# Constant products before the first attention block, a second bank and a later order for the products with v, and an earlier place for three attention blocks

## The chip, the cores and the metric

The kernel runs on one core of a Trainium2 chip. The metric is the device time of one execution in microseconds. One core has a matrix engine (PE), a vector engine (DVE), a scalar engine (ACT), GpSimd (POOL) and a queue engine (SP) that issues most transfers; each works through its own list in order and waits for the others by semaphores.

## What is computed

Three stages follow each other: causal attention with a decay, a layer norm with a two-layer MLP and a residual, and a gated MLP that mixes over the sequence. All of it is float32 with 4 batches, 8 heads, 576 positions and a head width of 64.

```python
scores = scale * np.matmul(q, k.transpose(0, 1, 3, 2))
decay = cum[:, :, :, None] - cum[:, :, None, :]          # cum: running sum of log f
scores = np.where(causal, -1e9, scores + decay)
attn = softmax(scores);  x = attn @ v                    # (4, 576, 512)
xn = (x - mu) / np.sqrt(var + 1e-06) * g_ln
x = x + np.maximum(xn @ w_ch1, 0.0) @ w_ch2              # 512 -> 2048 -> 512
h = np.maximum(x @ w_in, 0.0);  u, v = halves of h       # 512 -> 1024
out = (u * (w_spatial @ norm(v) + b_spatial)) @ w_out
```

## The kernel before

**Blocks.** The tokens are cut into eight blocks of 256 (`BLOCKS`, numbered 0 to 7) and the last 64 positions of each batch. Blocks 0 and 1 hold the first 128 positions of two batches each (`attention32`, float32 throughout), blocks 2 and 3 the next 128 (`attention1`), blocks 4 to 7 the positions from 256 on, one batch each (`attention`). Attention of each block goes over four pairs of heads (`p`, called pair 0 to 3 here). For each block the MLP follows as a group (`mlp`, numbered 0 to 7): sixteen rounds over tiles of the two weight matrices, L700 for the first product and L685 for the second. Group 0 runs in float32 while the weights are still being converted; the later ones in pairs of float16 parts.

**A pair of heads in `attention32`.** Scores (L352, four products into bank `acc`), row minimum on DVE (L355), exponentials on ACT (L357), the reciprocal of the sums and a diagonal matrix of it on DVE (L361, L365), a product with that (L369, bank `ph`) that transposes and scales, a copy on ACT (`PT`, L370), the product with v (L377, bank `av`, of which there is one) and its copy on ACT (`xT`, L378). After the fourth pair DVE adds the parts (`ls`), PE makes their mean (L603), and the norm and the first MLP group follow.

**A pair of heads in `attention`.** `weights(i, heads)` makes the scores of one tile of 128 rows (L293), the exponentials, and two float16 parts `P` on ACT (L258) and DVE (L314, the last of them); a transposing transfer writes them to `PT`. `values` multiplies with v (L456, thirty products) and is put, for one pair, behind the first tile's weights of the second head of the pair after it; for the last pair at the block's end.

**Weights.** Float64 weights arrive as 64-bit words (`raw`, 1 MB for each of sixteen tiles, three buffers). `narrow` makes float32 of them: ACT takes the high word (L525) and the low word (`low`, L526), DVE puts them together (L527 to L529), and PE makes sums of squares for the scales (`gram`, L561).

**What sets the order.** The program is written as an ordered list of events, each with a place in units of groups. `SPAN[n]` is the stretch in which block n's attention is placed, `BEGIN` the start of each group, `CONV` the conversions of the first weight tiles, `PACE` after what each conversion's first instruction is put. A scheduler then orders the instructions of each engine by its own timeline; `self.after(later, earlier)` forces one behind the other in that order without a wait at run time.

Of the kernel before, what the change touches and what calls it, by code (L numbers as in the profile page):

```python
# [9 lines left out]
BF16 = mybir.dt.bfloat16  # L10
I64 = mybir.dt.int64
U32 = mybir.dt.uint32
I32 = mybir.dt.int32
# [5 lines left out]
P = 128  # L19
# [18 lines left out]
W8 = 1  # L38
RAWB = 3
AHEAD = 2  # L40

# [7 lines left out]
E0, E1 = -0.1, 0.45  # L49
SPAN = [(-1.0, -0.6), (0.02, 0.45), (0.46, RAMP - 0.42), (RAMP - 0.4, RAMP - 0.1)]  # L50
for _n in range(4):
# [3 lines left out]
CONV = (-0.6, 0.001, 0.002, 0.003, 0.004)  # L55
PACE = (1, "split", "split", "split", "split")
SUMS = 13
SOON = 5
# [25 lines left out]
class Kernel:  # L84
# [194 lines left out]
    def weights(self, i, heads):  # L279
# [29 lines left out]
        for k0, k1 in pieces:  # L309
            w = P if k1 * P <= N else R  # L310
            src = sd[:M, k0 * P : k0 * P + (k1 - k0 - 1) * P + w].rearrange("p (t w) -> p t w", w=w)
            dh, dl = ph[:M, k0:k1, 0, :w], ph[:M, k0:k1, 1, :w]
            self.copy(DHE[i - 2], dh, src, rs)
            nc.vector.scalar_tensor_tensor(out=dl, in0=src, scalar=rs, in1=dh, op0=ALU.mult, op1=ALU.subtract)  # L314
        for u, (_, PT) in enumerate(heads):
            tr = nc.sync.dma_start_transpose(out=PT[:, : 2 * nb, qs], in_=ph[R * u : R * u + R, :nb].rearrange("p t h w -> p (t h w)"))
            self.in_order("tr", tr)


    def attention32(self, b, xT):  # L320
# [25 lines left out]
        for p in range(NP):  # L346
# [24 lines left out]
            if not b:  # L371
                self.done.append(copied)
            pav = bank(tags[2])
            for n in range(2):
# [65 lines left out]
    def attention(self, b, xT, xt):  # L440
# [5 lines left out]

        def values(p, vp, vsc, heads):

            pav = self.bank("av")
            for kt in range(5):  # L450
                n0 = max(kt * P, q0) - q0
                kr = min(P, S - kt * P)
                for vi, pi in ((0, 1), (1, 0), (0, 0)):
                    for u in range(2):
                        us = slice(64 * u, 64 * u + 64)
                        nc.tensor.matmul(  # L456
                            pav[us, n0:W], lhsT=vp[:kr, vi, kt, us], rhs=heads[u][1][:kr, 2 * kt + pi, n0:W],
                            start=(kt == 0 and (vi, pi) == (0, 1)), stop=(kt == 4 and (vi, pi) == (0, 0)), skip_group_check=True)
            nc.scalar.activation(xT[:, p, :], pav[:, :TOK], AF.Copy, scale=vsc)
            nc.scalar.activation(xt[:, p, :], pav[:, TOK:W], AF.Copy, scale=vsc)  # L460
            if p == 1:
                self.xs = self.mo_sum(xT)
            elif p == 2:
                nc.vector.tensor_tensor(out=self.xs, in0=self.xs, in1=xT[:, 2, :], op=ALU.add)
# [3 lines left out]
        for p in range(NP):  # L468
            heads = []
            for u in range(2):  # L470
# [7 lines left out]
                for i in (2, 3):  # L478
                    self.weights(i, heads[u:])
                    if late and (u, i) == (1, 2):  # L480
                        yield
                        values(*late)
                    yield
# [28 lines left out]
    def narrow(self, raw, tmp, low=None):  # L512
# [10 lines left out]
        else:  # L523

            first = nc.scalar.activation(a, words(raw, 1, F32), AF.Abs, scale=2.0**16)  # L525
            nc.scalar.activation(low.bitcast(I32), lo, AF.Copy, scale=LOW)  # L526
            nc.vector.tensor_scalar(out=a, in0=a, scalar1=F64_LO * 2.0**16, scalar2=F64_HI * 2.0**16, op0=ALU.max, op1=ALU.min)  # L527
# [14 lines left out]
    def load_w(self, j):  # L542
# [7 lines left out]
        if at is not None:  # L550
            self.after(first, self.marks[at] if isinstance(at, str) else self.done[at])

    def squares(self, j):
# [449 lines left out]
    def run(self):  # L1003
# [18 lines left out]
        at_cm = self.pool("at0", side="right")  # L1022
        self.at = at_cm.__enter__()
        with self.pool("dk") as dk:
            self.decays(dk)
# [208 lines left out]
```

## Time and profile before

| | us |
|---|---|
| median of three runs (lowest, highest) | 810.4 (809.69, 812.69) |
| the profiled execution, its own time | 811.59 |
| its span, first to last instruction | 809.9 |
| PE busy | 766.2 (95%) |
| DVE busy, ACT busy | 554.8 (69%), 516.7 (64%) |

A row of a timeline gives the start, the length, the engine with its line and the tiles written and read; in brackets stands how long the engine was idle before it and what ended that. Float32 products show two records each, so a row "x8" of L352 is the four products of one pair. Rows of one engine overlap a little, because products are pipelined: what a row takes in a stream is the distance from its start to the next row's. The granted clock of PE stands in the tables by stretch; 1.00 is 2.4 GHz and 0.50 is 1.2 GHz.

### The profile page before, as it was taken

What the parts mean: (1) busy time and instruction counts of PE and PEld (TensorE: products, weight loads), DVE (VectorE), ACT (ScalarE), POOL (GpSimd) and SP (SyncE); (2) the same over time, 40 slices, a digit from 0 to 9 for tenths busy, and PEclk for the clock granted to TensorE, in tenths of its full rate; (3) what the DMA queues carried; (4) which work ended last, traced back from release to release, by engine and by line L of the source; (5) the groups of instructions that cost most, each with busy time, mean ns of one, the idle gap of its engine ahead of it and who ended that gap; (6) DMA issues with size and microseconds to landing.
All of it is one profiled execution on the core that took longest, in us unless ns stands there. A gap on an engine that the chain in (4) does not pass through costs nothing.

```text
span 809.9 us, 16194 instructions
## 1 busy us (share of the span) xinstructions
PE 766.2 (95%) x5924; PEld 582.1 (72%) x5924; DVE 554.8 (69%) x1502; ACT 516.7 (64%) x1303; POOL 59.7 (7%) x89
## 2 busy tenths in 40 slices
PE   4889998999889999999999999999999999999997
PEld 4678887777777777877778788644447667667676
DVE  4479769938479988979757963778435563664735
ACT  4488668839478988878767862576325644656542
POOL 3000011001110101101101100100012000000000
PEclk9989999999999999999999999999999999999999
DMA  8578758336778998998787675651024230000101
GB/s 251 135 256 303 245 167 153 76 95 143 123 208 174 202 209 157 181 198 181 155 153 154 110 117 146 162 172 53 0 48 77 67 118 1 30 30 4 57 2 58
DMA packets 164226, 104.71 MB, mean 129 GB/s; under 512 B 106178, under 2 KB 151362, under 8 KB 164148
## 3 DMA queue, kind: packets, MB, share of 16 engines
q1 hardware_dynamic: 157848, 96.63, 49.0%
q0 software_dynamic: 5296, 5.28, 5.1%
q10 hardware_dynamic: 1004, 1.78, 0.8%
q8 instruction: 46, 0.75, 0.4%
q14 instruction: 32, 0.26, 0.1%
HBM read 64.37 MB, written 15.11 MB: 98 GB/s over the span
## 4 chain that ended last, share of the span: by engine, by line
PE 65%; DMA 11%; DVE 10%; ACT 9%; issue 3%; SPq 2%; POOL 1%; ACTq 0%; DVEq 0%; POOLq 0%
PE ph L700 14%; PE acc L685 13%; PE pb L640 8%; PE pb L641 8%; PE pb L642 8%; DMA PT<-P 5%; PE s L293 3%; PE av L456 3%; DMA vr<-in_v_dram 2%; DVE wt L593 2%; PE av L377 1%; PE s L685 1%; ACT x L258 1%; ACT P L258 1%; DMA raw<-in_moe_w_in_dram 1%
## 5 line engine op out<-in xcount | busy, mean ns | idle before, releaser
L685 PE MATMUL acc<-hh,wt 128*128 128x256 f16 (+2 forms) x960 | 196.7, 295 | 1.0 <-ACT hh L707 1.0
L700 PE MATMUL ph<-xh,wt 128*128 128x256 f16 (+1 forms) x896 | 185.6, 288 | 3.1 <-DVE hl L711 3.1
L700 PEld LDWEIGHTS <-wt 128*128 128x128 f16 x1344 | 126.9, 98 | 48.1 <-issue 9.6
L685 PEld LDWEIGHTS <-wt 128*128 128x128 f16 x1344 | 128.7, 98 | 44.7 <-issue 6.1
L700 PE MATMUL ph<-xl,wt 128*128 128x256 f16 (+1 forms) x448 | 129.0, 288 | 0.0
L685 PE MATMUL acc<-hl,wt 128*128 128x256 f16 (+1 forms) x416 | 115.4, 281 | 0.0
L707 ACT ACTIVATE hh<-ph 128x256 f16<-128x256 f32 (+2 forms) x128 | 51.0, 399 | 51.5 <-PE ph L700 51.3
L711 DVE SCALAR_TENSOR_TENSOR hl<-ph,hh 128x256 f16<-128x256 f32 (+1 forms) x112 | 50.5, 453 | 41.2 <-ACT hh L707 40.9
L258 ACT ACTIVATE P<-sd,st 128x512 f16<-128x512 f32 (+2 forms) x128 | 70.9, 586 | 8.0 <-DVE st L304 4.6
L301 ACT ACTIVATE sd<-sd,st 128x384 f32<-128x384 f32 (+2 forms) x80 | 54.6, 682 | 18.0 <-DVE st L297 17.8
L293 PE MATMUL s<-x 68*128 68x384 f32 (+7 forms) x256 | 63.3, 359 | 1.4 <-ACT sd L301 1.0
L314 DVE SCALAR_TENSOR_TENSOR P<-sd,st,P 128x384 f16<-128x384 f32 (+2 forms) x96 | 58.3, 625 | 8.7 <-ACT P L258 7.2
L297 DVE CUSTOM_DVE_ANT_0 sd<-s,mask 128x384 f32<-128x384 f32 (+2 forms) x80 | 46.0, 581 | 8.7 <-PE s L293 7.7
L732 POOL DMA_DIRECT2D x_d<-t x36 | 32.4, 1082 | 195.3 <-DVE t L728 169.5
L258 ACT ACTIVATE x<-qk 64x320 fp32r<-64x320 f32 (+1 forms) x64 | 41.6, 697 | 3.3 <-DMA qk<-in_qk_dram 2.0
L456 PE MATMUL av<-PT,vp 128*64 128x320 f16 (+2 forms) x480 | 33.9, 270 | 8.1 <-DMA PT<-P 6.4
L293 PEld LDWEIGHTS s<-x 68*128 68x128 f32 (+3 forms) x256 | 36.8, 177 | 4.3 <-ACT sd L301 1.2
L456 PEld LDWEIGHTS <-vp 128*64 128x64 f16 (+1 forms) x480 | 24.5, 109 | 19.5 <-issue 10.6
L983 DVE SCALAR_TENSOR_TENSOR u<-pb,wsc,u 128x288 f32<-128x288 f32 x32 | 15.9, 514 | 32.9 <-PE pb L982 32.9
L642 PE MATMUL pb<-x2h,wih 128*128 128x288 f16 (+2 forms) x144 | 37.8, 273 | 0.0
L640 PE MATMUL pb<-x2h,wil 128*128 128x288 f16 (+2 forms) x144 | 37.8, 273 | 0.0
L641 PE MATMUL pb<-x2l,wih 128*128 128x288 f16 (+2 forms) x144 | 37.8, 273 | 0.0
(275 smaller groups left out, 1619.8 us busy)
## 6 DMA issues: line engine op xcount, KB each, us to landing
raw<-in_moe_w_ch_dram SPq DMA_DIRECT2D x32, 512.0 KB
qk<-in_qk_dram SPq DMA_DIRECT2D x32, 448.0 KB
vraw<-in_v_dram SPq DMA_DIRECT2D x5, 1024.0 KB
vr<-in_v_dram SPq DMA_DIRECT2D x16, 320.0 KB
x_d<-xT SPq DMA_DIRECT2D x9, 512.0 KB
x_d<-t POOLq DMA_DIRECT2D x36, 128.0 KB, 4.3
out_dram<-o SPq DMA_DIRECT2D x32, 144.0 KB
raw<-in_moe_w_in_dram SPq DMA_DIRECT2D x8, 512.0 KB
```

The lines of the kernel that those rows point to most:

```text
L258: self.nc.scalar.activation(out, in_, AF.Copy, scale=scale)
L293: nc.tensor.matmul(ps[: R * u + R, : c1 - c0], lhsT=x[:, lo - q0 - R * u : hi - q0], rhs=y[:, c0:c1], start=g == 0, stop=g == len(heads[u] ...
L301: nc.scalar.activation(sd[:M, :N], sd[:M, :N], AF.Exp, bias=st[:M, n : n + 1], scale=-1.0, accum_out=st[:M, 2:3])
L314: nc.vector.scalar_tensor_tensor(out=dl, in0=src, scalar=rs, in1=dh, op0=ALU.mult, op1=ALU.subtract)
L456: nc.tensor.matmul(pav[us, n0:W], lhsT=vp[:kr, vi, kt, us], rhs=heads[u][1][:kr, 2 * kt + pi, n0:W], start=(kt == 0 and (vi, pi) == (0, 1) ...
L640: first = mm(out, lhsT=al, rhs=bh, start=start, stop=False, **kw)
L641: mm(out, lhsT=ah, rhs=bl, start=False, stop=False, **kw)
L642: mm(out, lhsT=ah, rhs=bh, start=False, stop=stop, **kw)
L685: ins = nc.tensor.matmul(acc[m], lhsT=a, rhs=b, start=bank not in clear, stop=last and e == len(terms) - 1, skip_group_check=True)
L700: ins = nc.tensor.matmul(ph, lhsT=a, rhs=b, start=k == e == 0, stop=k == NK - 1 and e == len(terms) - 1)
L707: relu = nc.scalar.activation(hh, ph, AF.Relu)
L711: nc.vector.scalar_tensor_tensor(out=hl, in0=ph, scalar=0.0, in1=hh, op0=ALU.max, op1=ALU.subtract)
```

## The change

There are five edits. **Constant products:** ahead of everything else on PE, 54 products of a tile of ones with itself (bfloat16, 128 by 128 against 256 columns) go into bank `s2`; nothing reads them. **Second bank:** in block 0, pairs 1 and 3 put the product with v into `s2` instead of `av`. **Later values:** in `attention`, the products with v of one pair are put behind DVE's last instruction (L314) of the first tile's weights of the second head of the next pair. **Low words:** the low-word conversions of weight tiles 0, 1 and 2 are put behind the copies `PT` of pairs 1, 2 and 3 of block 0 (`self.done`). **Places:** `SPAN` of block 1 ends 0.1 group sooner, blocks 2 and 3 begin 0.1 sooner, and blocks 4 to 7, whose places follow from block 3's end, 0.08 sooner.

```diff
+WARM = 54
-SPAN = [(-1.0, -0.6), (0.02, 0.45), (0.46, RAMP - 0.42), (RAMP - 0.4, RAMP - 0.1)]
+SPAN = [(-1.0, -0.6), (0.02, 0.35), (0.36, 0.98), (1.0, 1.32)]
+LOWAT = (1, 2, 3)
@@ weights
-            nc.vector.scalar_tensor_tensor(out=dl, in0=src, scalar=rs, in1=dh, op0=ALU.mult, op1=ALU.subtract)
+            low = nc.vector.scalar_tensor_tensor(out=dl, in0=src, scalar=rs, in1=dh, op0=ALU.mult, op1=ALU.subtract)
...
+        return low
@@ attention32
-            pav = bank(tags[2])
+            pav = bank("s2" if p % 2 and not b else tags[2])
@@ attention
-        def values(p, vp, vsc, heads):
+        def values(p, vp, vsc, heads, behind=None):
...
+                        if behind is not None and kt == 0 and (vi, pi) == (0, 1):
+                            self.after(ins, behind)
...
-                    self.weights(i, heads[u:])
+                    done = self.weights(i, heads[u:])
                     if late and (u, i) == (1, 2):
                         yield
-                        values(*late)
+                        values(*late, done)
@@ narrow
-            nc.scalar.activation(low.bitcast(I32), lo, AF.Copy, scale=LOW)
+            self.low = nc.scalar.activation(low.bitcast(I32), lo, AF.Copy, scale=LOW)
@@ load_w
+        if j < len(LOWAT):
+            self.after(self.low, self.done[LOWAT[j]])
@@ run
+        warm, ones = self.bank("s2"), self.ones.bitcast(BF16)
+        for i in range(WARM):
+            self.nc.tensor.matmul(warm[:, : 2 * P], lhsT=ones[:, :P], rhs=ones, start=True, stop=True)
```

The order of the instructions shows three places; a row that only repeats one above it is left out. The lines of the changed kernel are numbered a little higher: L352, L357, L369, L370, L377 and L526 of before are L355, L360, L372, L373, L380 and L531 there, L293 and L456 are L295 and L459, and L700 and L685 are L707 and L692.

PE from its first instruction, before: the scores of the four pairs of block 0, the transposing products of pairs 0 and 1, pair 0's products with v, pair 2's transposing products, the first scores of block 1 (`s2_447`) and pair 1's products with v.

```order
L352 MATMUL acc_169<-qk_151 128x128 x4
L352 MATMUL acc_201<-qk_151 128x128 x4
L352 MATMUL acc_235<-qk_151 128x128 x4
L352 MATMUL acc_268<-qk_151 128x128 x4
L369 MATMUL ph_187<-diag_171,e_170 128x128 x4
L369 MATMUL ph_219<-diag_203,e_202 128x128 x4
L377 MATMUL av_195<-PT_188,vr_152 128x128
L377 MATMUL av_195<-PT_188,vr_152 64x128
L369 MATMUL ph_253<-diag_237,e_236 128x128 x4
L352 MATMUL s2_447<-qk_431 128x128 x4
L377 MATMUL av_227<-PT_220,vr_152 128x128
L377 MATMUL av_227<-PT_220,vr_152 64x128
```

PE in the changed kernel, from the last of the 54 constant products on:

```order
L1033 MATMUL s2_93<-ones_62 128x256
L355 MATMUL acc_224<-qk_206 128x128 x4
L355 MATMUL acc_256<-qk_206 128x128 x4
L355 MATMUL acc_290<-qk_206 128x128 x4
L355 MATMUL acc_323<-qk_206 128x128 x4
L372 MATMUL ph_242<-diag_226,e_225 128x128 x4
L372 MATMUL ph_274<-diag_258,e_257 128x128 x4
L380 MATMUL av_250<-PT_243,vr_207 128x128
L380 MATMUL av_250<-PT_243,vr_207 64x128
L372 MATMUL ph_308<-diag_292,e_291 128x128 x4
L380 MATMUL s2_282<-PT_275,vr_207 128x128
L380 MATMUL s2_282<-PT_275,vr_207 64x128
```

The constant products stand ahead, and where block 1's scores stood behind pair 2 there are now pair 1's products with v, in the second bank, with pair 2's right behind; block 1's scores have gone behind the last product of block 0, just ahead of the mean.

ACT in block 0, before, from the exponentials of pair 1 on (`low` and `wt` are the conversions, `raw_160` the first weight tile):

```order
L357 ACTIVATE e_202,st_204<-e_202,st_204 128x128 x4
L526 ACTIVATE low_322<-raw_160 128x1024
L360 ACTIVATE st_204<-st_204 128x4
L357 ACTIVATE e_236,st_238<-e_236,st_238 128x128 x4
L360 ACTIVATE st_238<-st_238 128x4
L370 ACTIVATE PT_188<-ph_187 128x512
L526 ACTIVATE low_342<-raw_163 128x1024
L357 ACTIVATE e_269,st_271<-e_269,st_271 128x128 x4
L370 ACTIVATE PT_220<-ph_219 128x512
L525 ACTIVATE wt_146<-raw_160 128x1024
L378 ACTIVATE xT_150<-av_195 128x256
L360 ACTIVATE st_271<-st_271 128x4
```

ACT in the changed kernel, from the same exponentials on:

```order
L360 ACTIVATE e_257,st_259<-e_257,st_259 128x128 x4
L363 ACTIVATE st_227<-st_227 128x4
L360 ACTIVATE e_291,st_293<-e_291,st_293 128x128 x4
L363 ACTIVATE st_259<-st_259 128x4
L363 ACTIVATE st_293<-st_293 128x4
L373 ACTIVATE PT_243<-ph_242 128x512
L360 ACTIVATE e_324,st_326<-e_324,st_326 128x128 x4
L373 ACTIVATE PT_275<-ph_274 128x512
L530 ACTIVATE wt_201<-raw_215 128x1024
L531 ACTIVATE low_377<-raw_215 128x1024
L363 ACTIVATE st_326<-st_326 128x4
L381 ACTIVATE xT_205<-av_250 128x256
```

The first low word, which stood right behind the exponentials of pair 1, has gone behind the copy `PT` of pair 1, with the high word now ahead of it; the exponentials of pairs 2 and 3 and two copies `PT` stand ahead of both.

PE at the first product with v of pair 0 of block 4, before (`av_2668`; `s_2752` are scores of pair 1's last tile, in the middle of MLP products):

```order
L685 MATMUL acc_2477<-hh_3176,wt_146 128x256
L685 LDWEIGHTS wt_146
L685 MATMUL acc_2477<-hl_3177,wt_146 128x256
L456 LDWEIGHTS vp_2504
L456 MATMUL av_2668<-PT_2304,vp_2504 64x320
L293 MATMUL s_2752<-x2_2536 128x288
L293 MATMUL s_2752<-x1_2535 128x288
L293 MATMUL s_2752<-x2_2402 64x288
L293 MATMUL s_2752<-x1_2401 64x288
L685 MATMUL acc_2478<-hl_3177,wt_146 128x256
```

PE at the same product in the changed kernel (`av_2648`; `s2_2809` are scores of the next tile, of another head):

```order
L295 MATMUL s2_2809<-x2_2592 128x384
L295 MATMUL s2_2809<-x1_2591 128x384
L707 LDWEIGHTS wt_201
L707 MATMUL ph_3470<-xl_2607,wt_201 128x256
L707 MATMUL ph_3470<-xh_2606,wt_201 128x256
L692 LDWEIGHTS wt_201
L692 MATMUL acc_2608<-hl_3379,wt_201 128x256
L692 MATMUL acc_2608<-hh_3378,wt_201 128x256
L459 LDWEIGHTS vp_2462
L459 MATMUL av_2648<-PT_2301,vp_2462 64x320
L459 MATMUL av_2648<-PT_2366,vp_2462 64x320
```

The products with v (rows 2559 to 2618 of that list) now stand behind that next head's scores and five MLP products, and no longer in the middle of the last tile's scores.

## Rows read from the trace of the kernel before

**Rows 1.** busy time by stretch: us, busy us of PE, PEld, DVE, ACT, POOL, granted clock, DMA

```profile
50.00:100.00 50.00, 50.00 (x330) 43.30 (x329) 45.48 (x76) 38.56 (x72) 0.00 (x0) 1.00 0.80 278
```

**Rows 2.** PE's timeline: start us, length us, line, tiles, records, idle time before and its releaser

```profile
10.13 5.49 PE L352 MATMUL acc<-qk 66*128 66x128 f32 x24 [10.13 <-DMA qk<-decay]
16.08 2.05 PE L352 MATMUL acc<-qk 66*128 66x128 f32 x8 [0.46 <-DVE st L355]
...
21.56 2.05 PE L369 MATMUL ph<-diag,e 128*128 128x128 f32 x8 [1.73 <-DVE st L361]
23.40 2.60 PE L377 MATMUL av<-PT,vr 128*128 128x128 f32 x8
25.93 2.08 PE L369 MATMUL ph<-diag,e 128*128 128x128 f32 x8
28.43 2.05 PE L352 MATMUL s<-qk 66*128 66x128 f32 x8 [0.42 <-DMA qk<-decay]
...
32.80 1.03 PE L561 MATMUL gram<-wt 128*128 128x128 bf16 x8
...
38.26 1.63 PE L377 MATMUL av<-PT,vr 128*128 128x128 f32 x8 [0.47 <-ACT xT L378]
40.83 1.22 PE L603 MATMUL av<-ls,onesf 128*128 128x256 f32 x2 [0.93 <-DVE ls L614]
...
48.83 0.63 PE L561 MATMUL gram<-wt 128*128 128x128 bf16 x8 [0.83 <-DVE wt L529]
...
57.23 1.10 PE L369 MATMUL s<-diag,e 128*128 128x128 f32 x8
58.18 1.06 PE L352 MATMUL s<-qk 66*128 66x128 f32 x8
...
76.10 1.53 PE L377 MATMUL av<-PT,vr 128*128 128x128 f32 x8
```

**Rows 3.** busy time by microsecond, columns as in Rows 1, around the clock's first fall and rise

```profile
40.00:41.00 1.00, 0.17 (x1) 0.18 (x2) 0.42 (x1) 0.31 (x1) 0.00 (x0) 0.90 0.17 14
41.00:42.00 1.00, 1.00 (x2) 0.33 (x2) 0.00 (x0) 0.00 (x0) 0.00 (x0) 0.50 1.13 100
...
47.00:48.00 1.00, 0.98 (x2) 0.50 (x2) 0.96 (x2) 1.00 (x2) 0.00 (x0) 0.69 0.50 71
```

**Rows 4.** the chain of waits: start us, length us, what

```profile
9.34 6.62 DMA raw<-in_moe_w_ch_dram
```

**Rows 5.** ACT's timeline behind the exponentials of pair 1 of block 0

```profile
18.22 1.12 ACT L526 ACTIVATE low<-raw 128x1024 int32<-128x1024 uint32 x1 [2.11 <-DMA raw<-in_moe_w_ch_dram]
```

**Rows 6.** DVE's timeline at the kernel's start: the tile of ones

```profile
1.05 0.17 DVE L134 MEMSET ones<- 128x128 f32 x1
```

**Rows 7.** groups of ACT by line between 10 and 40 us: count, busy, mean ns

```profile
L357 ACT ACTIVATE e<-e,st 128x128 f32<-128x128 f32 x16 | 6.2, 390 | 2.8 <-DVE st L355 2.8
L526 ACT ACTIVATE low<-raw 128x1024 int32<-128x1024 uint32 x3 | 3.4, 1125 | 2.1 <-DMA raw<-in_moe_w_ch_dram 2.1
...
L370 ACT ACTIVATE PT<-ph 128x512 f32<-128x512 f32 x4 | 2.4, 590 | 4.0 <-PE ph L369 4.0
```

**Rows 8.** groups of DVE by line between 10 and 40 us

```profile
L528 DVE SCALAR_TENSOR_TENSOR low<-raw,low 128x1024 uint32<-128x1024 uint32 x3 | 3.7, 1221 | 2.8 <-ACT low L526 2.8
L365 DVE TENSOR_TENSOR diag<-ident,st 128x512 f32<-128x512 f32 x4 | 2.8, 688 | 0.1
...
L529 DVE SCALAR_TENSOR_TENSOR wt<-wt,low 128x1024 uint32<-128x1024 uint32 x1 | 1.2, 1195 | 0.0
```

**Rows 9.** waits of PE between 100 and 460 us: total, times, longest

```profile
PE av L456 <- DMA PT<-P: 6.4, 7, 1.7
PE av L428 <- DMA PT<-P: 4.6, 3, 1.7
```

**Rows 10.** PE's timeline: products with v of pair 3 of blocks 5 and 6

```profile
353.73 0.32 PE L456 MATMUL av<-PT,vp 128*64 128x320 f16 x1 [0.68 <-DMA PT<-P]
...
420.36 0.30 PE L456 MATMUL av<-PT,vp 128*64 128x320 f16 x1 [1.22 <-DMA PT<-P]
```

More of the change, by code (lines that the diff above doesn't have):

```diff
@@ L455, in values @@
                         us = slice(64 * u, 64 * u + 64)
-                        nc.tensor.matmul(
+                        ins = nc.tensor.matmul(
                             pav[us, n0:W], lhsT=vp[:kr, vi, kt, us], rhs=heads[u][1][:kr, 2 * kt + pi, n0:W],
                             start=(kt == 0 and (vi, pi) == (0, 1)), stop=(kt == 4 and (vi, pi) == (0, 0)), skip_group_check=True)
+                        if behind is not None and kt == 0 and (vi, pi) == (0, 1):
+                            self.after(ins, behind)
             nc.scalar.activation(xT[:, p, :], pav[:, :TOK], AF.Copy, scale=vsc)
```

## The prediction

> **What bounds the kernel now.** I read the table by stretch first. From 50 to 100 us PE is busy without a gap [rows 1], while the start has limits of its own. PE's own list bounds the kernel, so time comes only from work that PE does before its unbroken stream, and from gaps in it. The stream starts at 48.83 us and the mean ahead of it at 40.83 us; the 8.0 us between are a chain through DVE, ACT and PE that the change leaves alone [rows 2]. So I ask when the mean of block 0 can start, and then what becomes of PE's gaps.
>
> Next is PE's timeline of the start. Three pairs' scores take 5.49 us from 10.13, or 1.83 for each; a pair's transposing products take 1.84 at 21.56 and its products with v 2.53 at 23.40, from one row's start to the next. Rows of the same sets later last 1.06, 1.10 and 1.53 us, where these last 2.05, 2.05 and 2.60 [rows 2]. So PE runs at half speed here, 1.2 GHz. The granted clock reads 1.00 until its first recorded fall to 0.50, between 40 and 41 us, and comes back between 47 and 48 us [rows 3]; before 40 us I go by the lengths, and by them the clock rises once, shortly before the row of 38.26 us, whose 1.63 us are nearly the fast 1.53. Ahead of that rise PE had worked from 28.43 to 37.8 us. The 5.49 us of scores from 10.13 had not raised it, nor had the run from 21.56 to 28.0 [rows 2].
>
> Third are the gaps at the start. Pair 3's scores begin at 16.08 us; the bracket names DVE, but the chain has a transfer landing at 9.34 + 6.62 = 15.96 us there [rows 2, 4]. ACT stood 2.11 us at the first low word, waiting for weights, and gave 1.12 us to it [rows 5], ahead of pair 1's sums; PE lost 1.73 us before 21.56 for this. Another 0.47 us went before 38.26 for the single bank `av` [rows 2].
>
> **The constant products.** The trace has no such product. In `gram`, 128 columns eight times take 1.03 us at the low clock and 0.63 at the high one [rows 2], tails of 0.2 us included, so 256 columns are about 0.21 or 0.11 us (estimates). All 54 would take 11.3 or 5.9 us. They can start at about 1.3 us, when the ones are written [rows 6]. With a rise 4 to 6 us later some 19 to 28 are slow, and they end between 9 and 10.2 us, beside transfers that hold PE until 10.13 anyway [rows 2]. Cost nothing, then; 2.5 us of delay for the first scores if the clock never rose. What they buy is that the first scores run at the high clock.
>
> **Does the clock stay?** Pairs 0 and 1 then need 2.1 us from 10.13; pair 2 ran at 10.13 + 2 x 1.83 = 13.8 in before, and pair 3 still waits for 16.0. PE is thus half idle between 12 and 16 us. In before the clock fell at 40.9 us behind gaps of 0.47 and 0.93 us, with PE busy for 0.17 of its last microsecond [rows 2, 3]. By that row I take it that the clock is lost between 13 and 17 us. The Trainium skill (TensorE: Matmul & The Clock Gate, HAM oscillation) shows the clock lost to waits of 3 to 5 us between bursts. None of the gaps here would be that long, and by it the clock would stay high all through, which is rival (b). The fall at 40.9 us speaks against it.
>
> **The mean of block 0, two bounds.** From 16.0 us on PE has one set of scores, four transposing sets, four with v, one `gram` and block 1's first scores. At the low clock that is 1.83 + 4 x 1.84 + 4 x 2.53 + 0.84 + 1.83 = 22.0 us, so the mean starts at 38.0. This holds if nobody keeps PE waiting: the low word and its wait now stand behind `PT` of pair 1, and `s2` takes pairs 1 and 3. At the high clock PE's work is 11 to 12 us, and another chain is later. Pair 3's exponentials cannot begin before 17.3; ACT has four of them at 0.39 us, two `PT` of 0.59 and the high and low word of 1.12 each [rows 7], to 22.3. DVE's L528, L529 and the diagonal follow, 1.22 + 1.20 + 0.69 [rows 8], to 25.4. Then come PE's 0.95, `PT` 0.59, PE's 1.45, the copy `xT` and the sum, some 0.4 each (estimates, `PT` is twice as wide), with nine hand-overs at about 0.15 us: the mean at about 31.
>
> Between them: PE works from 16.0 without a break in this order, and a run of 9 us from 28.43 brought the clock up. So it rises at about 25; 9 of 22 us are done by then, the other 13 take 7, which gives 32, and ACT's chain adds about 1. I take **33.1**, against 40.83: **7.7 us sooner**, of bounds 2.8 and 9.8. A part may be lost again: the norm's chain leaves PE mostly idle, so the stream may start at the low clock, where in before the rise came just ahead of it. I take 1.0 us back (bounds 0 and 2, half of up to 4 us).
>
> **The stream.** In it the MLP rows and block 1's pairs keep their order to within a few products, and loads and conversions go by its pace, so I carry the whole shift through. DVE is busy 45.5 of 50 us there [rows 1], close, but PE has no gap.
>
> **Later values.** PE waited 6.4 us, seven times, for `PT` at products with v in blocks 4 to 7, at most 1.7 us [rows 9]. In the new order the first three pairs of each block have 1.9 to 9.3 us more of PE work between their last scores and the products with v, 4.7 in the mean (PE's order, summed with the durations of the rows). The mean is well above the longest wait, so those waits are gone; the last pair of a block keeps its place and its wait, 0.68 and 1.22 us of the 6.4 [rows 10]. I take **4.5 us** (bounds 0 and 6.4).
>
> **Places.** In block 2 two products with v now stand 1.4 and 2.0 us closer behind their scores. Transfers of `PT` held three such products for 4.6 us in before [rows 9], so closer ones can wait: I take **1.5 us** as loss (bounds 0 and 3.4). The other moves change no distance by as much; cost nothing, within 1.5 either way.
>
> Sum: 7.7 - 1.0 + 4.5 - 1.5 = 9.7 us. The profiled execution took 811.6 us, 1.7 of them outside its span, and would become 801.9; it stands 1.2 above the median of 810.4, against which I predict **800.7**.
>
> **Rivals.** (a) *The clock stays low until 38 us:* sets with v ran in the stretches that did not raise it. Then the mean comes at 38.0, 2.8 sooner, with nothing lost at the stream: 2.8 + 4.5 - 1.5 = 5.8, **804.6**. (b) *It stays high from the constant products on,* because the gaps are short: the mean at 31, 9.8 + 4.5 - 1.5 = 12.8, **797.6**. (c) *The constant products do not raise it:* they end at 12.6 us, pairs 0 to 2 follow at the low clock until 18.1, pair 3 until 19.9 in place of 17.8, the mean is at 40.1: 0.7 + 4.5 - 1.5 = 3.7, **806.7**. (d) *Slower:* products with v that come later also free `PT` later. If the transposing transfers of the pair after next wait for that, SP's queue stands with every load behind it, and each of twelve moved products meets a wait. At 1.7 us, the longest seen [rows 9], that is 20.4 us in place of the 4.5 gained: 7.7 - 1.0 - 1.5 - 20.4 = -15.2, **825.6**. It decides the sign from 5.2 / 12 = 0.4 us for each. Against it speaks that two pairs of `PT` alternate and the products still stand ahead of the weights that reuse them.
>
> **How the numbers follow.** The forecast gets 0.50, (a) 0.22, (b) 0.14, (c) 0.08, (d) 0.06. About 0.5%, 4.1 us, is what a measurement can tell from no change here, so faster means below 806.3. Nearly all of the forecast, whose unknown costs put it at 797 to 805.5, (b), and three quarters of (a) lie below: 0.81 faster, 0.13 within, 0.06 slower. The range holds the forecast, (b) with no loss in block 2 (796.1) and (a) with half of the values' gain (806.9): 795.5 to 807.5.
>
> **What would show it.** Right: 54 products that end before 10.2 us and get shorter on the way; scores of pairs 0 and 1 in about 1.05 us each; no wait of ACT at the first low word; the mean near 33 us and the stream's first `gram` near 41; waits for `PT` at the values' line of about 2 us in place of 6.4. Wrong: a mean at 38 us (the clock) or at 31 (it stayed), a stream that starts earlier but has new gaps, or waits on SP's queue for the products with v.

## The result: about 9 us faster, near the forecast, for reasons that were partly others

| | kernel before | changed kernel |
|---|---|---|
| median, same job | 811.55 us (809.69 to 813.18, 4 runs) | 801.67 us (800.36 to 804.47, 4 runs) |
| ratio to before | 1 | 0.9884, interval 0.9846 to 0.9922 |
| profiled execution, its span | 811.6, 809.9 us | 800.8, 799.1 us |
| mean of block 0 starts | 40.83 us | 31.35 us |
| first transposing set inside the stream | 57.23 us | 49.09 us |
| PE waits for `PT` at the values' line | 6.4 us, 7 times | 2.2 us, once |
| PE waits for anything at that line | 8.1 us, 9 times | 4.9 us, 3 times |
| PE waits for `PT` at attention1's products with v | 4.6 us, 3 times | 0.3 us, once |

The forecast was 800.7 us, with a range of 795.5 to 807.5. All lines of the changed kernel stand a few numbers lower down: L355 are the scores (L352 before), L372 the transposing products, L380 block 0's products with v, L459 the later blocks' (L456), L610 the mean (L603), L707 and L692 the MLP, L1033 the constant products.

PE's timeline of the changed kernel's start, columns as in [rows 2]:

```profile
8.76 0.49 PE L1033 MATMUL s<-ones 128*128 128x256 bf16 x3
10.16 2.05 PE L355 MATMUL acc<-qk 66*128 66x128 f32 x16 [0.91 <-DMA qk<-decay]
12.72 1.13 PE L355 MATMUL acc<-qk 66*128 66x128 f32 x8 [0.51 <-DVE st L358]
14.26 1.13 PE L355 MATMUL acc<-qk 66*128 66x128 f32 x8 [0.41 <-DVE st L358]
16.24 3.75 PE L372 MATMUL ph<-diag,e 128*128 128x128 f32 x16 [0.85 <-ACT e L360]
19.79 2.60 PE L380 MATMUL av<-PT,vr 128*128 128x128 f32 x8
22.32 1.16 PE L372 MATMUL ph<-diag,e 128*128 128x128 f32 x8
...
30.22 1.16 PE L355 MATMUL s<-qk 66*128 66x128 f32 x8
31.35 0.67 PE L610 MATMUL av<-ls,onesf 128*128 128x256 f32 x2
...
39.01 0.77 PE L568 MATMUL gram<-wt 128*128 128x128 bf16 x8 [1.12 <-DVE wt L534]
39.57 3.53 PE L707 MATMUL ph<-xg,wt 128*128 128x256 f32 x8
...
45.12 1.94 PE L707 MATMUL ph<-xg,wt 128*128 128x256 f32 x8
46.90 1.89 PE L692 MATMUL acc<-hh,wt 128*128 128x256 f32 x8
```

All four pairs' scores are done by 15.4 us, where before pair 3 began only at 16.08 [rows 2]. From 16.24 on PE goes through four pairs almost without a break, and block 1's first scores come behind all of them instead of ahead of pair 1's products with v. The row of 39.57 has eight records, which are four MLP products, in 3.53 us; in the next round, at the high clock, four take 1.94, or 1.78 to the start of the row behind them.

The clock in the changed kernel, busy time by microsecond, columns as in [rows 1]; the granted clock is the last number but two:

```profile
15.00:16.00 1.00, 0.39 (x4) 0.20 (x2) 0.78 (x2) 1.00 (x6) 0.00 (x0) 0.73 1.19 391
16.00:17.00 1.00, 0.76 (x3) 0.79 (x4) 0.34 (x4) 0.86 (x6) 0.00 (x0) 0.50 0.97 396
...
22.00:23.00 1.00, 1.00 (x8) 0.69 (x7) 0.58 (x1) 1.00 (x2) 0.00 (x0) 0.86 1.12 191
...
39.00:40.00 1.00, 0.99 (x9) 1.00 (x10) 1.00 (x2) 1.00 (x7) 0.00 (x0) 0.68 1.11 426
...
42.00:43.00 1.00, 1.00 (x5) 0.79 (x4) 1.00 (x3) 1.00 (x2) 0.00 (x0) 0.62 1.00 384
```

It falls from 2.4 to 1.2 GHz at about 15.5 us, returns at about 22.3, falls again as the stream begins and returns at about 42.8 us. Later it falls five more times, near 132, 196, 234, 288 and 408 us, each time for a little over three microseconds. The last four microseconds apart, before had one such fall behind its start, at 645 us.

PE's waits in the stretch in which blocks 2 to 7 have their attention, total, times, longest; these answer to [rows 9], and two rows of the same view of the kernel before (100 to 460 us) stand ahead of them, since they are at the same line:

```profile
PE av L456 <- ACT P L258: 1.1, 1, 1.1
...
PE av L456 <- PE s L293: 0.6, 1, 0.6
```

The changed kernel (105 to 478 us):

```profile
PE ph L707 <- DVE hl L718: 2.8, 3, 1.6
PE av L459 <- DMA PT<-P: 2.2, 1, 2.2
PE av L459 <- ACT x L260: 1.7, 1, 1.7
PE s L295 <- DMA x<-decay_d: 1.7, 2, 1.0
...
PE av L459 <- ACT sd L303: 1.0, 1, 1.0
...
PE av L431 <- DMA PT<-P: 0.3, 1, 0.3
```

### The profile page after: what moved, and what is told of

It is laid out like the page before. It is cut to its first block, busy times and chain, and to the rows that moved or that the text cites. A ratio compares the mean times of both kernels' runs of the same rounds, so it can differ in the third digit from the quotient of the medians.

```text
span 799.1 us, 16326 instructions
## 1 busy us (share of the span) xinstructions
PE 770.2 (96%) x5978; PEld 584.1 (73%) x5978; DVE 555.1 (69%) x1502; ACT 516.0 (65%) x1303; POOL 60.8 (8%) x89
## 3 DMA queue, kind: packets, MB, share of 16 engines
q10 hardware_dynamic: 1004, 1.78, 0.7%
## 4 chain that ended last, share of the span: by engine, by line
PE 75%; DVE 9%; ACT 6%; DMA 6%; issue 3%; POOL 1%; SPq 1%; ACTq 0%; DVEq 0%; POOLq 0%
PE ph L707 20%; PE acc L692 16%; PE pb L647 8%; PE pb L648 8%; PE pb L649 8%; PE s L295 4%; PE s L692 3%; PE av L459 3%; DMA PT<-P 2%; DMA vr<-in_v_dram 2%; DVE wt L600 2%; PE av L380 1%; ACT x L260 1%; DMA qk<-in_qk_dram 1%; PE gram L568 1%
## 5 line engine op out<-in xcount | busy, mean ns | idle before, releaser
L692 PE MATMUL acc<-hh,wt 128*128 128x256 f16 (+2 forms) x960 | 198.6, 297 | 1.6 <-ACT hh L714 1.4
L707 PE MATMUL ph<-xh,wt 128*128 128x256 f16 (+1 forms) x896 | 189.1, 293 | 2.8 <-DVE hl L718 2.8
L707 PEld LDWEIGHTS <-wt 128*128 128x128 f16 x1344 | 129.1, 99 | 48.5 <-issue 8.7
L692 PEld LDWEIGHTS <-wt 128*128 128x128 f16 x1344 | 130.1, 99 | 46.7 <-issue 7.4
L707 PE MATMUL ph<-xl,wt 128*128 128x256 f16 (+1 forms) x448 | 131.0, 293 | 0.0
L692 PE MATMUL acc<-hl,wt 128*128 128x256 f16 (+1 forms) x416 | 116.8, 284 | 0.2 <-DVE hl L718 0.2
L295 PE MATMUL s<-x 68*128 68x384 f32 (+7 forms) x256 | 62.7, 359 | 2.4 <-DMA x<-decay_d 1.7
L295 PEld LDWEIGHTS s<-x 68*128 68x128 f32 (+3 forms) x256 | 36.9, 177 | 5.7 <-DVE st L299 1.5
L459 PE MATMUL av<-PT,vp 128*64 128x320 f16 (+2 forms) x480 | 32.6, 278 | 4.9 <-DMA PT<-P 2.2
L647 PE MATMUL pb<-wsh,vl 128*128 128x288 f16 x128 | 36.6, 286 | 0.2 <-DVE x2s L204 0.2
```

The source lines that it names most:

```text
L295: nc.tensor.matmul(ps[: R * u + R, : c1 - c0], lhsT=x[:, lo - q0 - R * u : hi - q0], rhs=y[:, c0:c1], start=g == 0, stop=g == len(heads[u] ...
L459: ins = nc.tensor.matmul(pav[us, n0:W], lhsT=vp[:kr, vi, kt, us], rhs=heads[u][1][:kr, 2 * kt + pi, n0:W], start=(kt == 0 and (vi, pi) == ...
L647: first = mm(out, lhsT=al, rhs=bh, start=start, stop=False, **kw)
L692: ins = nc.tensor.matmul(acc[m], lhsT=a, rhs=b, start=bank not in clear, stop=last and e == len(terms) - 1, skip_group_check=True)
L707: ins = nc.tensor.matmul(ph, lhsT=a, rhs=b, start=k == e == 0, stop=k == NK - 1 and e == len(terms) - 1)
```

## Experiments

Each run has its own runs of the kernel before on the same chip. Those gave medians of 809.39 us (19 runs), 809.2 (14) and 806.84 (17) in the three jobs, and spread from 802.3 to 815.6 us, so single medians tell little under 4 us. A time within a start, such as that of the mean, is read from one execution of each kernel. How far it moves by itself is shown by `e9`: up to the mean it has the order of the kernel before on PE, ACT, DVE and SP, and its mean comes 2.65 us sooner.

| run | median us (runs) | ratio to before, interval | mean of block 0, us |
|---|---|---|---|
| e1_no_products | 800.09 (4) | 0.9879, 0.9802 to 0.9956 | 31.91 |
| e2_values_early | 803.52 (10) | 0.9922, 0.9887 to 0.9957 | 32.26 |
| e3_old_places | 792.84 (4) | 0.9789, 0.9724 to 0.9854 | 32.42 |
| e4_products_alone | 805.55 (10) | 0.9946, 0.9911 to 0.9981 | 41.05 |
| e5_low_free | 801.82 (4) | 0.9889, 0.9845 to 0.9933 | 34.32 |
| e6_one_bank | 812.81 (10) | 1.0042, 1.0016 to 1.0068 | 39.09 |
| e8_old_places_no_products | 794.68 (4) | 0.9809, 0.9769 to 0.9850 | 32.37 |
| e9_places_alone | 816.38 (5) | 1.0086, 1.0059 to 1.0114 | 38.18 |
| e10_end_kept | 800.76 (4) | 0.9909, 0.9873 to 0.9945 | 32.30 |
| e11_end_alone | 794.03 (4) | 0.9838, 0.9805 to 0.9871 | 31.51 |
| e12_end_later | 801.59 (6) | 0.9924, 0.9894 to 0.9954 | 31.30 |
| e13_end_latest | 809.65 (12) | 1.0023, 1.0001 to 1.0045 | 32.99 |

### What shortens the start

**Without the constant products** (changed kernel, one number):

```diff
-WARM = 54
+WARM = 0
```

> The changed kernel without its 54 constant products; everything else stays. If the granted clock is what shortens the start, pairs 0 to 2 take 1.8 us each again, PE works at the low clock from 10.1 us on and the mean of block 0 starts at 36 to 38 us instead of 31.4, so the time is 5 to 7 us over the changed kernel's (806 to 809). If the order alone shortens it (ACT no longer stands at the first low word, the second bank), the mean starts by 33 us and the time stays within 2 us of the changed kernel's.

The time is that of the changed kernel (0.9879 against 0.9884), and the mean comes only 0.56 us later. PE's timeline of this run says why:

```profile
9.98 7.28 PE L355 MATMUL acc<-qk 66*128 66x128 f32 x32 [9.98 <-DMA qk<-decay]
17.05 3.62 PE L372 MATMUL ph<-diag,e 128*128 128x128 f32 x16
20.46 1.75 PE L380 MATMUL av<-PT,vr 128*128 128x128 f32 x8
22.15 1.16 PE L372 MATMUL ph<-diag,e 128*128 128x128 f32 x8
```

All four pairs' scores (32 records) run at the low clock, but without a gap, end at 17.26, and PE goes straight on. By the lengths of the rows the clock is up by about 20.5 us, nearly two microseconds earlier than with the products, which had made the scores short and PE idle between them. Scores that are done sooner wait longer for exponentials.

Nor do the products always give the scores their clock. In `e2`, which has the changed kernel's order at the start, they end at 8.83 us, the transfer for the first scores lands 1.55 us behind them, the clock falls to 0.50 within the next row, and most of the scores run slow:

```profile
10.38 6.58 PE L355 MATMUL acc<-qk 66*128 66x128 f32 x32 [1.55 <-DMA qk<-decay]
```

```profile
11.00:12.00 1.00, 1.00 (x8) 1.00 (x8) 0.10 (x1) 0.00 (x0) 0.00 (x0) 0.60 1.15 183
```

**The products alone**, in the kernel before:

```diff
+WARM = 54
...
+        for i in range(WARM):
+            self.nc.tensor.matmul(warm[:, : 2 * P], lhsT=ones[:, :P], rhs=ones, start=True, stop=True)
```

> The kernel before with the 54 constant products and nothing else. If the clock needs the other edits to bring anything (ACT still stands at the first low word, the bank av is single), the mean starts at 37 to 40 us and the time is 1 to 3 us under the kernel before. If the clock alone makes the start short, the mean starts by 34 us and the time is 6 us or more under the kernel before.

The mean stays where it was, at 41.05 us. PE is through its first sets sooner and then stands in front of block 1's scores, which here still come ahead of pair 1's products with v, for a transfer:

```profile
29.55 2.05 PE L353 MATMUL s<-qk 66*128 66x128 f32 x8 [4.61 <-DMA qk<-decay]
```

The run is 4.4 us faster than before all the same (0.0054 of 810; by its interval 1.5 to 7.2), though its stream begins later: the first transposing set in it starts at 59.82 us instead of 57.23. Behind the start the two have the same order on SP, and on PE, ACT and DVE but for a step or two that neighbours have swapped. What this run gains, it gains behind its start (PE loses 16.9 us in the attention of blocks 2 to 7, against 20.0 in before, by the table below), and nothing in its start explains that.

**Without the pinned low words:**

```diff
-LOWAT = (1, 2, 3)
+LOWAT = ()
```

> The changed kernel without the three waits that put the low words behind PT of pairs 1 to 3. If the pinned low words shorten the start (ACT stood 2.1 us at the first one in the kernel before), the mean of block 0 comes 1.5 to 2.5 us later, near 33.5, and the time is 803 to 804. If the second bank alone does it, the mean stays within 0.5 us of 31.4 and the time within 1.5 us of 801.7.

ACT waits for weights at the first low word again, ahead of work for PE:

```profile
17.64 1.12 ACT L531 ACTIVATE low<-raw 128x1024 int32<-128x1024 uint32 x1 [1.84 <-DMA raw<-in_moe_w_ch_dram]
```

The mean comes 2.97 us later than in the changed kernel. Part of that is a transfer: pair 3's scores, in an order that is the same up to there, waited for theirs until 15.42 us, against a start at 14.26 in the changed kernel. The median is no different (0.9889), within an interval of 0.4% either way; the profiled spans differ by 2.6 us. So a cost of the free low words isn't shown in the time, and their 3 us at the mean are hardly more than what a start moves by itself.

**With one bank** for block 0's products with v:

```diff
-            pav = bank("s2" if p % 2 and not b else tags[2])
+            pav = bank(tags[2])
```

> The changed kernel with one bank for block 0's products with v. In its order block 1's first scores stand ahead of pairs 2 and 3 again, as in the kernel before. If the bank (and the order that comes of it) carries the shorter start, these scores wait for their transfer at about 28 us and the mean comes at 35 to 38: 805 to 809. If the pinned low words carry it, the mean stays at 31.5 to 33 and the time at 801 to 804.

This is the costliest edit to take back: 1.0042 against 0.9884, 12.8 us, and nearly 4 us above the range expected. The scheduler then puts block 1's first scores ahead of pair 1's products with v, and PE stands there for their transfer:

```profile
26.92 1.13 PE L355 MATMUL s<-qk 66*128 66x128 f32 x8 [3.23 <-DMA qk<-decay]
...
39.09 0.70 PE L610 MATMUL av<-ls,onesf 128*128 128x256 f32 x2 [0.97 <-DVE ls L621]
```

The mean comes 7.7 us later than in the changed kernel, and 6.8 us later than in `e2`, which goes by the same times as `e6` up to 22.5 us. The wait for the transfer is 3.23 us of that; at about 28.2 us, 1.3 us behind it, the clock falls, and it is low for 6.8 us. So the second bank carries the shorter start, by these rows less by the idle time at the bank itself (0.47 us, here as in [rows 2]) than by the order that the scheduler makes of it: no work that waits for a late transfer stands in front of block 0's own. A kernel with one bank and the changed kernel's order, which would show that alone, was not run, and of the 12.8 us the 5 that the mean doesn't show are not traced.

### The later values

```diff
-                        values(*late, done)
+                        values(*late)
```

> The changed kernel with the products with v of blocks 4 to 7 put where they were before; everything else stays. If their later place saves what PE waited for PT, waits of that line for PT come back to 5 to 8 us from 2.2 and the time rises by 3 to 5 us (805 to 807). If gaps there cost nothing in the end, or the later place only moved the waits to other lines, the time stays within 1.5 us of the changed kernel's.

3.1 us slower than the changed kernel by the ratios (0.0038 of 810), with intervals that overlap. The profile has `PT` waits of 5.7 us, three times, at the values' line, against 2.2 once; with waits for anything else at that line it is 7.7 against 4.9 us. Right in sign, and the size is uncertain.

### The places

```diff
-SPAN = [(-1.0, -0.6), (0.02, 0.35), (0.36, 0.98), (1.0, 1.32)]
+SPAN = [(-1.0, -0.6), (0.02, 0.45), (0.46, RAMP - 0.42), (RAMP - 0.4, RAMP - 0.1)]
```

> The changed kernel with the places of blocks 1 to 3 as before; everything else stays. If the places are worth nothing, as I took it (or a loss of 1.5 us), the time is 800 to 803 and attention1's products with v wait for PT for under 1 us in all. If the places are what took 4 us of waits from block 2's products with v, those waits come back to 3 to 5 us and the time rises by 3 to 5 us.

The changed kernel with the old places takes 792.84 us: 0.0095 of 810, 7.7 us, faster than with the new ones, and the fastest of all that ran. Neither expectation foresaw that; attention1's products with v wait 1.5 us for `PT`, once. To tell a cost of the places from an accident of one order, I took them back without the products, and added them alone to the kernel before.

The first has, on the changed kernel, the edit above and

```diff
-WARM = 54
+WARM = 0
```

> The changed kernel with the old places of blocks 1 to 3 and without the 54 products. Theory 1 (the earlier places cost by themselves, some 7 to 9 us, whatever runs at the start): as the changed kernel without products took 800.1 and the old places with products 792.8, this takes 791 to 794. Theory 2 (792.8 was the luck of where the clock's falls met work in that one order; the places move time only by that): about 800, as without the products, within 2 us. Either way the mean of block 0 near 32 us.

The second has, on the kernel before,

```diff
-SPAN = [(-1.0, -0.6), (0.02, 0.45), (0.46, RAMP - 0.42), (RAMP - 0.4, RAMP - 0.1)]
+SPAN = [(-1.0, -0.6), (0.02, 0.35), (0.36, 0.98), (1.0, 1.32)]
```

> The kernel before with the earlier places of blocks 1 to 3 and nothing else. Theory 1 (the places cost 7 to 9 us by themselves): 816 to 819 against 809.4. Theory 2 (no cost of their own): 807 to 812. Rival 3 (they cost only together with the later products with v, since both bring a block's products closer to the next block's): 807 to 812 as well, and old places without later products would then not gain. The start is that of before: mean near 41 us.

Both go by theory 1 (`e8` by 0.7 us beside its range). The start of `e9` came sooner than that of before, though its order was the same:

```profile
38.18 1.14 PE L603 MATMUL av<-ls,onesf 128*128 128x256 f32 x2 [0.93 <-DVE ls L614]
...
54.52 1.11 PE L369 MATMUL s<-diag,e 128*128 128x128 f32 x8
```

Its stream's first transposing set stands 2.7 us ahead of before's, and the run is slower all the same: the loss lies behind the start. Without products the old places are 5.7 us faster than the new (0.9879 and 0.9809); alone the new places make the kernel before 7.0 us slower. So three pairs of kernels put their cost at 5.7 to 7.7 us, and the last of them, by its stream, at more.

The place of the loss is the stretch with the attention of blocks 2 to 7. Here are single rows over it, from the changed kernel, from `e3` and from `e9`:

```profile
105.00:478.00 373.00, 359.56 (x3208) 293.51 (x3207) 296.75 (x832) 285.10 (x762) 38.63 (x52) 0.98 0.78 156
```

```profile
106.00:477.00 371.00, 359.01 (x3280) 296.28 (x3278) 298.11 (x835) 285.37 (x764) 37.86 (x52) 1.00 0.80 157
```

```profile
112.00:491.00 379.00, 357.97 (x3208) 291.91 (x3206) 298.64 (x832) 285.16 (x761) 38.25 (x52) 0.98 0.75 153
```

PE is idle for 13.4, 12.0 and 21.0 us, and granted 0.98, 1.00 and 0.98 of its clock. Adding the clock's deficit by microsecond to the idle time gives what PE loses there:

| order | idle + clock in the stretch, us | sum |
|---|---|---|
| before | 20.0 + 0 | 20.0 |
| e4 (old places) | 13.5 + 3.4 | 16.9 |
| e9 (new places, values early) | 21.0 + 6.8 | 27.8 |
| changed kernel (new) | 13.4 + 8.5 | 22.0 |
| e1 (new) | 18.4 + 0 | 18.4 |
| e10 (new, end kept) | 15.7 + 5.1 | 20.8 |
| e3 (old) | 12.0 + 1.7 | 13.7 |
| e8 (old) | 10.8 + 0 | 10.8 |
| e11 (old, end sooner) | 14.1 + 0 | 14.1 |

With later values, new places lose 18 to 24 us here (`e5` 21.8 and `e6` 24.1, worked out in the same way) and old ones 11 to 14 (`e12` 11.3, `e13` 14.1). Idle time and low clock partly replace each other (the changed kernel and `e1` have the same order on PE, but for the constant products), so a fall of the clock isn't simply added.

My next theory was that attention takes its time whatever its place, and that only the MLP work left behind it counts. In PE's order 634 MLP products stand behind the last product with v in the changed kernel and 559 in `e3`, and the time from there to the end is 321.4 and 315.1 us. Two kernels separate the ends of that stretch from the places of blocks 2 and 3: the first keeps the new places of blocks 1 to 3 and the old end,

```diff
-    SPAN.append((SPAN[-1][1], SPAN[-1][1] + 2.35 / 4))
+    SPAN.append((SPAN[-1][1], SPAN[-1][1] + 2.43 / 4))
```

> The changed kernel with its earlier places of blocks 1 to 3, but blocks 4 to 7 spread over 2.43 groups in place of 2.35, so that the last block's attention ends at 3.75 groups as in the kernel before. 563 MLP products stand behind the last product with v in its order, against 634 in the changed kernel and 559 with the old places. Theory 1 (attention takes its time from other engines, and what counts is how much MLP work is left behind it): 792 to 795, tail 315 to 316 us. Rival (the nearer places of blocks 2 and 3 cost by waits of their own): 799 to 802.

the second has the old places and the new end:

```diff
-SPAN = [(-1.0, -0.6), (0.02, 0.35), (0.36, 0.98), (1.0, 1.32)]
+SPAN = [(-1.0, -0.6), (0.02, 0.45), (0.46, RAMP - 0.42), (RAMP - 0.4, RAMP - 0.1)]
...
-    SPAN.append((SPAN[-1][1], SPAN[-1][1] + 2.35 / 4))
+    SPAN.append((SPAN[-1][1], SPAN[-1][1] + 2.27 / 4))
```

> The changed kernel with the old places of blocks 1 to 3, but blocks 4 to 7 spread over 2.27 groups, so that the last attention ends at 3.67 groups as in the changed kernel. 640 MLP products stand behind the last product with v. Theory 1 (what counts is the MLP work left behind): 799 to 803, tail 321 to 323 us. Rival (the places of blocks 2 and 3 themselves): 792 to 795.

The theory falls, and the rival holds: 800.76 us with the new places and the old end, 794.03 with the old places and the new end. In `e11` attention ends 8.6 us sooner than in `e3` (468.6 and 477.2 us) and the rest is 8.8 us longer (323.9 and 315.1). MLP work moved across the end of attention costs and gains nothing, since PE does it on either side.

What the new places cost is thus in blocks 1 to 3, and what follows from their order. One step of it can be named. Before the first product with v of block 6's last pair PE waits 1.22 us for `PT` in the kernel before [rows 10], and 0.23, 1.22, 1.95 and 0.92 in `e3`, `e8`, `e11` and `e12` (old places; the 1.95 is put down to issue), but 2.21 in the changed kernel, and 1.86, 3.06, 3.74, 2.01 and 3.98 in `e1`, `e2`, `e5`, `e6` and `e10`. The rows of the changed kernel and of `e10`:

```profile
407.64 0.30 PE L459 MATMUL av<-PT,vp 128*64 128x320 f16 x1 [2.21 <-DMA PT<-P]
```

```profile
409.00 0.45 PE L459 MATMUL av<-PT,vp 128*64 128x320 f16 x1 [3.98 <-DMA PT<-P]
```

On average that is 2.8 against 1.1 us, and in four of the six the clock falls during the wait or right behind it, for 1.7 us of work or more. So in the kernels with later values it is some 3 of the 6 to 8 us (an estimate from these waits and falls). It isn't the whole, and not everywhere: `e9`, with new places and values early, and `e13`, with old places, have no wait there at all. The others lie at different lines in each kernel (in `e9` the longest is a load of `decay_d`, 4.52 us at 411.70 us). Why these transfers come later with the new places stays open.

**Later still.** If the end is free to move, does more MLP work beside attention help?

Both have the old places of blocks 1 to 3, as `e3`.

```diff
-    SPAN.append((SPAN[-1][1], SPAN[-1][1] + 2.35 / 4))
+    SPAN.append((SPAN[-1][1], SPAN[-1][1] + 2.45 / 4))
```

> The changed kernel with the old places of blocks 1 to 3 and blocks 4 to 7 spread over 2.45 groups: the last attention ends at 3.85, 478 MLP products stand behind it, 81 fewer than with the old places. At 0.109 us each these are 8.8 us. Theory 1, while attention still takes as long: 784 to 787, tail about 307 us. If attention's stretch is by now bound by PE, it grows by what is moved into it: 791 to 794.

The same with 2.55 in place of 2.45:

```diff
-    SPAN.append((SPAN[-1][1], SPAN[-1][1] + 2.35 / 4))
+    SPAN.append((SPAN[-1][1], SPAN[-1][1] + 2.55 / 4))
```

> As the run before, with the last attention ending at 3.95: 428 MLP products behind it, 131 fewer than with the old places, 14.3 us. PE's gaps and clock losses in attention's stretch were 13 us in all with the old places, so not all of it can be gained: theory 1 gives 780 to 786 with a stretch that grows by 3 to 8 us; if nothing more is to be gained behind the 3.85, 784 to 788; if the last block's MLP rows then wait for their input, 788 to 795.

No. Both times are above every range expected (801.59 and 809.65 us). The stretch grows by what is moved into it (378.5 and 386.2 us, against 371.0 in `e3`), and then the last block's MLP rows wait for their input. In `e12`, and twice in `e13`:

```profile
504.51 1.01 PE L707 MATMUL ph<-xh,wt 128*128 128x512 f16 x2 [5.02 <-ACT xh L668]
```

```profile
509.95 1.01 PE L707 MATMUL ph<-xh,wt 128*128 128x512 f16 x2 [5.79 <-ACT xh L668]
...
521.90 1.01 PE L692 MATMUL acc<-hh,wt 128*128 128x512 f16 x2 [4.72 <-ACT hh L714]
```

## Why the prediction was right, and where its steps were not

**The bound.** Right: PE's own list is the limit, and the mean's start sets the stream's. The mean came 9.48 us sooner, the stream's first `gram` 9.82, and its first transposing set, behind the cold start, 8.14; the path from mean to stream stayed a chain through DVE, ACT and PE.

**Constant products.** Cost nothing, as worked out: the last ends at 9.25 us, and the first scores wait for their transfer until 10.16. In the ten executions that have them, 13 to 26 of the 54 are slow and the last ends between 8.6 and 10.0 us. Pairs 0 and 1 take 1.03 us each, as predicted, where the clock lasts. But what they buy is nothing: rival (c) put the mean at 40.1 us without the raised clock, of which 2.5 are the slow products themselves, and `e1`, without products and without the raised clock, has it at 31.91. The failed step is the one that let the low clock go on to about 25 us or to the mean; by [rows 2] scores alone hadn't raised it, but in the new order work follows them at once, and in `e1` the clock is up by 20.5.

**Pair 3 waits for a transfer until 16.0.** Wrong. Its scores began at 14.26, released by DVE; in `e5` they did wait for a transfer, until 15.42, in an order that is the same up to there. The landing at 15.96 [rows 4] is that of a weight tile (`raw`), which the scores don't read, so it gave no floor; and the scores' own transfer comes at another time in each execution.

**The clock.** It was lost between 13 and 17 us, as taken from [rows 3]: at about 15.5, behind gaps of 0.51 and 0.41 us and as one of 0.85 began. So rival (b) did not hold here. The Trainium skill (TensorE: Matmul & The Clock Gate, HAM oscillation) tells of a clock lost to waits of 3 to 5 us; that shorter gaps keep it, as rival (b) read it, does not follow, and no gap here was longer than 0.91 us. That it held until 15.5 is partly chance: in `e2` and `e6`, with the same order up to there, it fell at 11.2. It came back at about 22.3 us instead of the 25 I took: the run from 28.43 in [rows 2] told that so long a one brings it back, not that a shorter one doesn't. These 2.7 us at full instead of half speed are worth some 1.35 us of work, most of the 1.75 us by which the mean (31.35, forecast 33.1) came sooner. Rival (a) is out too. In the fast bound the nine hand-overs were taken at 0.15 us each; in the trace of before an engine that waited for another mostly starts 0.03 to 0.10 us behind it.

**What shortens the start.** The sum contained the right order, block 1's scores last, but the text credited the raised clock and ACT's low word. The runs give the larger part to the second bank (7.7 us at the mean) and at most 3.0 us to the low words; together that is more than the shift of 9.5, so what one brings partly needs the other.

**The stream's cold start.** Right in kind: 3.53 us for four products, 1.7 us lost, of a range of 0 to 2; I had taken 1.0.

**Later values.** Waits for `PT` at their line went from 6.4 to 2.2 us (about 2 forecast), and the first three pairs of a block wait for nothing any more, where they had waited 4.9 us in all: the mechanism was right. But the last pairs, whose place the edit leaves alone, went from 3.3 to 4.9 us, part of it now put down to ACT (1.7 and 1.0 us, blocks 4 and 5) and 2.21 instead of 1.22 to block 6's `PT`. At the line 3.2 us are saved, near the 3.1 us of time by `e2`, of 4.5 forecast.

**Places.** The term that was mis-sized: 1.5 us, bounds 0 and 3.4, and the runs say 5.7 to 7.7. Its mechanism was wrong as well. Attention1's products with v were to wait more for `PT`; they wait 0.3 us in the changed kernel instead of 4.6, and with the places alone (`e9`) 3.6. I had compared distances on PE only between scores and their products with v, while the loss came up as waits for loads, for `PT` in blocks that hardly moved, and as low clock behind them.

**The sum.** By the runs it came out because two errors cancel, and that is luck. By differences of the ratios, the start's three edits are worth 13.3 us (`e9` to `e2`, 1.0086 and 0.9922), later values 3.1 (`e2` to the changed kernel), places -7.0 (before to `e9`): 9.4 in all. I had 6.7, 4.5 and -1.5. But little of the 13.3 is in the start itself, since `e9` had its stream early already. In `e2` it begins only 3.6 us sooner than in `e9`:

```profile
50.93 1.11 PE L372 MATMUL s<-diag,e 128*128 128x128 f32 x8
```

In the two profiled executions, whose spans are 814.4 and 804.6 us, the rest lies in the attention of blocks 2 to 7, where PE loses 6.1 us less in `e2` (21.7 and 27.8). `e4` shows the same in kind, 4.4 us with a stream that came later. Which transfer or engine then comes sooner, no run isolates. From before to the changed kernel, the profiled executions have 8.1 of their 10.8 us ahead of the stream's first transposing set.

**Rival (d)**, products with v that free `PT` late and stop SP's queue: not seen. No wait of that kind is longer than 2.21 us in the changed kernel.

## What to carry to other kernels

Look at what stands in a queue in front of the critical work and waits for a late transfer. A second bank was worth 13 us here, 7.7 of them seen at the end of block 0, and by the rows less for the half microsecond of waiting for the bank than because a scheduler with a free bank no longer fills the hole with such work. Time an edit of places or due times by itself, apart from the edits it comes with: it hid a loss of some 7 us inside a gain of 17 (0.9789), and leaving it out gives the best kernel measured (`e3`, 792.84 us). Where work is only moved along a list that PE does without a break anyway, as at the end of attention in `e10` and `e11`, expect nothing from it. And read a difference of one or two microseconds within a start from more than one execution: the same order moved by 2.65 us here.

## What the hardware showed that I had not expected

The same order does or doesn't lose its clock behind the same gap. The changed kernel and `e1` have the same order on PE behind the start, and each waits 0.72 us for DVE's `hl` near 132 us. In the changed kernel the clock is at half in the microsecond that follows:

```profile
131.69 0.37 PE L707 MATMUL ph<-xh,wt 128*128 128x256 f16 x1 [0.72 <-DVE hl L718]
```

```profile
132.00:133.00 1.00, 1.00 (x7) 0.67 (x6) 1.00 (x3) 1.00 (x4) 0.00 (x0) 0.50 0.69 175
```

In `e1` it stays:

```profile
133.15 0.27 PE L707 MATMUL ph<-xh,wt 128*128 128x256 f16 x1 [0.72 <-DVE hl L718]
```

```profile
133.00:134.00 1.00, 0.85 (x8) 0.77 (x8) 1.00 (x4) 1.00 (x5) 0.00 (x0) 1.00 0.37 46
```

In the attention of blocks 2 to 7 the changed kernel lost its clock five times, in or behind gaps of 0.4 to 2.2 us, `e1` not once behind gaps up to 2.0 us. So a single gap's length doesn't tell whether the clock goes. One fall in a busy stretch costs about 1.7 us of work, which is the size of many of the differences that one would like to explain here.

Equal orders also differ more than expected: the kernel before alone spread over 12 us in one job (802.34 to 814.36, 19 runs), with nothing changed.
